# A gated recurrence and its feed-forward on one core: two-batch chunks, crossbar transposes a step earlier, and unequal weight slices

## Chip, cores and metric

The kernel runs on one core of a Trainium2 chip. The core has five engines with a queue each, executed in order: TensorE (PE, matmuls), VectorE (DVE), ScalarE (ACT), GpSimd (POOL) and SyncE (SP, which here only issues transfers). Sixteen DMA engines move data between memory and the core. The metric is the device time of one execution in microseconds (us), lower being better.

## What is computed

Two stages, one feeding the other. The first is a linear attention with a forget gate: for each of 4 batches and 8 heads, a 48 x 48 state is decayed row by row and updated at each of 768 positions, and read out by q. The second is a gated feed-forward without a bias, on rows of 8 x 48 = 384 values, with 1536 hidden units.

```python
f = 1.0 / (1.0 + np.exp(-f_logit))
for t in range(S):                       # S = 768
    state = f[:, :, t, :, None] * state + np.einsum('bhd,bhe->bhde', k[:, :, t], v[:, :, t])
    y[:, :, t] = np.einsum('bhd,bhde->bhe', q[:, :, t], state)
...
gate = np.maximum(x @ w_gate, 0.0)       # x: y as 3072 rows of 384
val = x @ w_val
return (gate * val @ w_out)
```

All inputs and the output are float32; the kernel casts the operands of its matmuls to bf16.

## The kernel before

**Attention in steps.** The 768 positions are cut into 6 steps of 128 (`c` = 0 to 5), and each step is done for the four batches `b` = 0 to 3. `attention(c, b)` works as follows. ACT turns the gate logits into logarithms (L570 and L573, two batches at a time). PE forms their running sums with a triangular matrix (L580, and the sum over the step at L582). ACT takes exponentials of them in both signs (L589, L591) and of the total (L595). POOL multiplies k and q by these, which gives the "hats" (L600, L603), and casts v into a padded tile (L556). The hats lie with positions on partitions and are needed the other way round. For steps below `first_xbar_qk` PE transposes them (L613, eight 128 x 128 transposes into one PSUM bank, copied out by DVE at L619); from that step on SP issues a transposing DMA through the crossbar (L622). Step 0 has a path of its own, `first_pair`. Then PE forms the scores (L636), DVE masks them (L642), and PE forms the output, from the old state (L671) and from the masked scores and v (L675). ACT copies it out (L689). It is transposed to xT by PE (L697, step 2 and below) or by DMA (L705, step 3 and above). PE forms the update of the state (L716), and DVE and POOL apply it (L730, L732).

**Feed-forward in chunks.** `ffn_hidden(c, b0, b1, j)` does one of 12 blocks of 128 hidden units for the batches b0 to b1 of step c: three matmuls for the gate, three for the value (both L748, with 128 columns per batch), a relu on ACT (L755) and a product on DVE (L759). `ffn_out` does the output rows of a batch: 12 matmuls (L770), a copy on ACT (L782) and a store by SP (L785). Which batches go together is listed in `groups`: (step, first batch, last batch, whether outputs follow at once). In the kernel before, step 1 goes in two chunks, and the others from step 2 on in one chunk of four batches, hence 512 columns per matmul. Step 0 is written out ahead of that loop: the weights come in `wsteps` = 3 slices of 4 blocks, and for each slice the two halves of the batches are done.

**Transfers.** SP issues all loads of f, k, q and v (L397, from step 1 on two batches in one load of 393 KB, in rows of 48 floats), the crossbar transposes and the stores, in one queue. POOL issues the loads of the weights, which cast to bf16 (L417). The list `early` fixes the order of the first loads and slices; each may wait until an earlier one of the other kind has landed. Inputs have three buffers (`NL`), so a load of step c waits for the use of step c - 3.

**The order.** Nothing is ordered by hand beyond that. All operations are recorded with `add`, with a cost (`occ`: the engine is taken; `lat`: until the result is there) and a priority, and `Plan.schedule` lists them on each engine by simulating these costs. Feed-forward matmuls have a low priority (1000 is added), so they fill PE wherever attention isn't ready by the plan. `settled` and `margin` add 0.5 us (PE) or 0.6 us (SP) to the readiness of what depends on other engines after 40 us of planned time, feed-forward matmuls excepted. Transfers have a planned flow (0.9 us per batch of a load, 1.06 per hat transpose). The plan only fixes orders: on the chip each engine runs its list and waits on semaphores. `NWARM` = 100 matmuls on zeros (L453) fill PE until the first feed-forward matmul.

Of the kernel before, what the change touches and what calls it, by code (L numbers as in the profile page):

```python
# [43 lines left out]
class Plan:  # L44
# [4 lines left out]
    def __init__(self, limits):  # L49
        self.ops = []  # L50
        self.limits = limits
        self.settled, self.margin = 0.0, {}

    def add(self, eng, emit, reads=(), writes=(), occ=0.5, lat=0.2, prio=0, opens=(), after=(), follows=(),
            paced=()):
# [39 lines left out]
    def schedule(self, banks):  # L95
# [25 lines left out]
        while left:  # L121
            pick = None
            for e in self.ENGINES:
                for op in waiting[e]:
                    at = max(free[e], op.ready)
                    slot = ()
                    if op.opens:
                        slot = banks_for(op)
                        if slot is None:
                            continue  # L130
                        at = max(at, slot[-1]["at"])
                    key = (at, op.prio, op.idx)
                    if pick is None or key < pick[0]:
                        pick = (key, op, slot)
            if pick is None:
                raise RuntimeError("no op can be scheduled: " + repr(
                    [(e, len(waiting[e])) for e in self.ENGINES]))
            (at, _, _), op, slot = pick
            e = op.eng
            waiting[e].remove(op)  # L140
            if op.ends:
                gone = {o for o in self.ops if o.filler and o.start is None}
                waiting["PE"] = [o for o in waiting["PE"] if o not in gone]
                self.ops = [o for o in self.ops if o not in gone]
                left -= len(gone)
            for tile, s in zip(op.opens, slot):
                if s["tile"] is not None:
                    for o in s["tile"].ops:
                        op.deps[o] = "war"
                s["tile"] = tile  # L150
                tile.ap, tile.slot = s["ap"], s
                used[tile.group] = used.get(tile.group, 0) + 1
            op.start, op.end = at, at + op.occ + op.lat
            if op.flow is not None:
                backlog = max(flow_free - op.end, 0.0)
                flow_free = op.end + backlog + op.flow
                op.end += op.flow + op.late + (min(backlog, op.flow) if op.ring == "own" else backlog)
            free[e] = at + op.occ
            op.pos = len(order[e])
            order[e].append(op)  # L160
            left -= 1
            for t in {t for t in op.reads + op.writes if isinstance(t, Bank)}:
                if all(o.start is not None for o in t.ops):
                    t.slot["at"] = max(o.end for o in t.ops)
                    used[t.group] -= 1
            for u in op.users:
                u.n_left -= 1
                if u.deps[op] == "order":
                    at = op.start
                elif u.eng == op.eng == "PE":  # L170
                    at = op.start + op.occ
                else:
                    at = op.end
                    if at > self.settled and (u.eng != "PE" or u.prio < 1000):
                        at += self.margin.get(u.eng, 0.0)
                u.ready = max(u.ready, at)
                if u.n_left == 0:
                    waiting[u.eng].append(u)
# [50 lines left out]
def bass_hgrn2_outer__then__ffn_reglu_kernel(  # L229
# [7 lines left out]
    w_out: bass.AP,  # L237
    out: bass.AP,
):
    wsteps = 3  # L240
    early = ("f0.0.1 f0.1.2 f0.2.3 f0.3.4 k0.0.1 k0.1.2 q0.0.1 q0.1.2 v0.0.1 v0.1.2 k0.2.3 k0.3.4 "
             "q0.2.3 q0.3.4 v0.2.3 v0.3.4 wg0 wv0 wg1 wv1 wg2 wv2 f1.0.2 k1.0.2 q1.0.2 v1.0.2 wo0 wo1 "
             "wo2 f1.2.4 k1.2.4 q1.2.4 v1.2.4").split()
    lag = 4.0
    first_xbar_qk = 3
    flight = 3
    WP = 0
    NWARM = 100
    split_first = 1
    late = 2.5  # L250
    spread_engines = ['ACT', 'DVE', 'ACT', 'ACT']
# [2 lines left out]
    first_xbar_x = 3  # L254
    load_batches = 2
    hat_engines = ['DVE', 'POOL']
    groups = [(0,0,4,1),(1,0,2,0),(1,2,4,0),(2,0,4,0),(3,0,4,0),(4,0,4,0),(5,0,4,0)]
    B, H, S, D = q.shape
    C = 128
    NC = S // C  # L260
# [2 lines left out]
    NK = HD // 128  # L263
# [52 lines left out]

    pl = Plan({"bc": 1, "tp": 1, "s": 2, "y": 1, "kv": 1, "f": 4, "w": 1})
    pl.settled, pl.margin = 40.0, {"PE": 0.5, "SP": 0.6}
    add = pl.add
    gp, ve, sc, te, sy = nc.gpsimd, nc.vector, nc.scalar, nc.tensor, nc.sync  # L320

# [31 lines left out]
        ["ident"], ["ident"], occ=0.3, prio=-8)  # L353
    add("POOL", lambda: gp.memset(ones[:], 1.0), [], ["ones"], occ=0.1, prio=-8)

    def zero(eng, e, t, name, cols, prio):
        add(eng, lambda: e.memzero(t), [], [name], occ=0.15 + cols / 2000.0, prio=prio)  # L357

    zero("DVE", ve, zeros[:], "zeros", 128, -20)
    for i in range(NB):  # L360
        zero("DVE", ve, bneg[i][:], f"bneg{i}", 1024, -9)
    for i in range(NH):
# [20 lines left out]
    def load(n, c, b0, b1, after=(), paced=(), eng="SP"):  # L383
        last = tails.get("load" + eng)
        e = sy if eng == "SP" else sc
        t = ld[n][c % NL]
        src = bass.AP(tensor=srcs[n].tensor, offset=b0 * H * S * D + c * C * D,
                      ap=[[D, C], [S * D, (b1 - b0) * H], [1, D]])
        dst = t[:, b0:b1, :, :].rearrange("p b h d -> p (b h) d")
        flow = 0.9 * (b1 - b0)  # L390
        if c == 0 and n != "v":
            u = b0 % 2
            src = bass.AP(tensor=srcs[n].tensor, offset=b0 * H * S * D, ap=[[2 * D, 64], [S * D, H], [1, 2 * D]])
            dst = t[64 * u:64 * u + 64, b0 - u:b0 - u + 2, :, :].rearrange("p b h d -> p (b h d)").rearrange(
                "p (h x) -> p h x", h=H)
            flow = 0.82
        op = add(eng, lambda: e.dma_start(dst, src), [], [f"{n}{c % NL}_{b}" for b in range(b0, b1)],  # L397
                 occ=(0.8 if eng == "SP" else 0.3) * (b1 - b0) * (0.8 if c == 0 else 1), lat=2.0 if c == 0 else 0.9, prio=c * 100 - 150 * (eng != "SP"), after=after,
                 follows=[last] if last else [], paced=paced)
        tails["load" + eng] = op  # L400
        dma(op, f"{n}{c % NL}_{b0}{b1}", flow, (6.0 if (c, n, b0) == (1, "v", 0) else 2.0) if c else 0.8)
        return op

    WJ = NJ // wsteps
    wsrc = {"wg": w_gate, "wv": w_val}

    def load_w(nm, s, after, landed=()):
        if nm == "wo":
            src = bass.AP(tensor=w_out.tensor, offset=s * WJ * 128 * DM,
                          ap=[[DM, 128], [128 * DM, WJ], [1, DM]])  # L410
            dst = wo[:, s * WJ:(s + 1) * WJ, :]
        else:
            src = bass.AP(tensor=wsrc[nm].tensor, offset=s * WJ * 128,
                          ap=[[DFF, 128], [128 * DFF, NK], [1, WJ * 128]])
            dst = (wg if nm == "wg" else wv)[:, :, s * WJ * 128:(s + 1) * WJ * 128]
        last = tails.get("load_w")
        op = add("POOL", lambda: gp.dma_start(dst, src), [], [f"{nm}{s}"], occ=0.8, lat=1.0, prio=WP, paced=after,  # L417
                 after=landed, follows=[last] if last else [])
        tails["load_w"] = op
        dma(op, f"{nm}{s}", 6.3 / wsteps)  # L420
        return op


# [26 lines left out]

    cold = Bank("w")
    for i in range(NWARM):
        op = add("PE", lambda: te.matmul(cold.ap[:, 0:256], zeros[:, 0:128], zeros[:, :]), ["zeros"], [cold], occ=0.22 if i < 17 else 0.11,  # L453
                 lat=PE_L, prio=1000000, opens=[cold] if i == 0 else [])
        op.filler = True

# [279 lines left out]
    def ffn_hidden(c, b0, b1, j):  # L736
# [8 lines left out]
        def proj(bank, wt):  # L745
            def run():
# [2 lines left out]
                                   start=(kt == 0), stop=(kt == NK - 1))  # L749
                return mm  # L750
            return run
        op = chain("ffn", "PE", proj(gate, wg), xk + [f"wg{j // WJ}"], [gate], occ=pe_t(n, n, n), lat=PE_L,
              prio=P + 1000, opens=[gate])
        op.ends = count["h"] == 1
        add("ACT", lambda: sc.activation(relu[ri][:, 0:n], gate.ap[:, 0:n], AF.Relu), [gate], [f"relu{ri}"],  # L755
            prio=P, **act_t(n))
        chain("ffn", "PE", proj(val, wv), xk + [f"wv{j // WJ}"], [val], occ=pe_t(n, n, n), lat=PE_L,
              prio=P + 1000, opens=[val])
        add("DVE", lambda: ve.tensor_tensor(gT[gi][:, j, n0:n1], relu[ri][:, 0:n], val.ap[:, 0:n], ALU.mult),  # L759
            [val, f"relu{ri}"], [f"gT{gi}_{j}_{b}" for b in range(b0, b1)], prio=P, **dve_t(n))  # L760
# [1 line left out]
    def ffn_out(g, *bs):  # L762
# [11 lines left out]
        for s in range(NJ // OJ):  # L774
            js = range(s * OJ, (s + 1) * OJ)
            for o, b in zip(outs, bs):
                P = (g + 1) * B * 10 + 5 + NJ * 3 + b * 3
                chain("ffn", "PE", proj_out(o, b, s), [f"gT{gi}_{j}_{b}" for j in js] + sorted({f"wo{j // WJ}" for j in js}),
                      [o], occ=pe_t(*[DM] * OJ), lat=PE_L, prio=P + 1000, opens=[o] if s == 0 else [])
        for o, b in zip(outs, bs):  # L780
            oi, P = (g * B + b) % NO, (g + 1) * B * 10 + 5 + NJ * 3 + b * 3
# [5 lines left out]
            dma(op, f"osb{oi}", 0.45)  # L787

    OJ = 4
    OPAIR = 2  # L790
    count = {"h": 0}
    sent = {x[1:] for x in early if x[0] != "w"}
# [3 lines left out]
    for c in range(NC):  # L796
# [7 lines left out]
        for b in range(B):  # L804
            attention(c, b)
        if c == 0 and split_first:
            for s in range(wsteps):
                for b0 in (0, 2):
                    for j in range(s * WJ, (s + 1) * WJ):
                        ffn_hidden(0, b0, b0 + 2, j)  # L810
            for b in range(0, B, OPAIR):
                ffn_out(0, *range(b, b + OPAIR))
# [92 lines left out]
```

## Time and profile before

| | before |
|---|---|
| time, median of 3 (lowest to highest) | 202.8 us (201.86 to 203.2) |
| profiled span | 198.9 us |
| busy: PE, ACT, DVE, POOL | 192.1, 115.1, 107.0, 77.2 us |
| loads of f, k, q, v from issue to landing, medians | 5.2 to 5.8 us |
| transpose of hats by DMA, issue to landing, median | 3.9 us |
| granted TensorE clock | 1.000 |

The profiled execution is a separate one, and its span is counted from its first to its last instruction, so it lies below the timed executions. Busy PE time counts overlapping matmuls once, but the end of a matmul is modelled; what a matmul costs in a row of others is read from the distance between starts. A row of the timeline gives the start, the length, the engine, the line and operation, the tiles written and read, and in brackets the engine's idle time before it with what ended it.

### The profile page before, as it was taken

How to read it: one execution, taken by the hardware profiler on the slowest of the kernel's cores; microseconds unless marked ns; L12 is line 12 of the kernel's file. 1: busy time of each engine (PE TensorE's matmuls, PEld its weight loads, DVE VectorE, ACT ScalarE, POOL GpSimd, SP SyncE). 2: the span in 40 equal slices, each digit the busy share in tenths (PEclk: the TensorE clock that was granted, in tenths of full speed). 3: DMA queues.
4: the chain of work that ended last, by engine and by line, in shares of the span. 5: the costliest groups of instructions: out<-in, count | busy, mean ns of one | idle time of the engine just before them, and what ended most of it. 6: DMA issues, size and time to landing. Idle time of an engine off the chain costs nothing.

```text
span 198.9 us, 4530 instructions
## 1 busy us (share of the span) xinstructions
PE 192.1 (97%) x1796; PEld 122.9 (62%) x1796; DVE 107.0 (54%) x208; ACT 115.1 (58%) x263; POOL 77.2 (39%) x111
## 2 busy tenths in 40 slices
PE   7999999999999999999997989999999999999994
PEld 5887588866888787745553535555545555544552
DVE  7258865574399787647737443636265233443300
ACT  2786767906888677867649466386425433344311
POOL 5189303733859668693573174504500000000000
PEclk9999999999999999999999999999999999999999
DMA  4999999999979999999798899988942200111112
GB/s 118 232 225 198 201 214 187 209 222 243 254 173 227 193 240 177 198 212 207 158 213 167 174 185 202 215 171 187 190 112 59 63 31 9 40 40 43 40 71 87
DMA packets 118180, 31.74 MB, mean 160 GB/s; under 512 B 111248, under 2 KB 118160, under 8 KB 118160
## 3 DMA queue, kind: packets, MB, share of 16 engines
q1 hardware_dynamic: 114176, 27.93, 70.3%
q0 software_dynamic: 3984, 3.54, 11.2%
q8 instruction: 14, 0.23, 0.5%
q14 instruction: 6, 0.05, 0.1%
HBM read 25.95 MB, written 4.72 MB: 154 GB/s over the span
## 4 chain that ended last, share of the span: by engine, by line
PE 78%; DMA 10%; SPq 5%; ACT 3%; POOL 2%; issue 1%
PE ps L748 43%; PE ps L770 22%; SPq L397 4%; DMA wv<-in_moe_w_val_dram 4%; PE ps L636 3%; DMA q_in<-in_q_dram 3%; DMA f_in<-in_f_logit_dram 2%; DMA k_in<-in_k_dram 2%; PE ps L613 2%; PE ps L675 2%; PE ps L716 2%; PE ps L671 2%; PE ps L580 1%; ACT relu L755 1%; POOL hats L603 1%; PE ps L582 1%
## 5 line engine op out<-in xcount | busy, mean ns | idle before, releaser
L759 DVE TENSOR_TENSOR gT<-relu,ps 128x256 bf16<-128x256 bf16 (+1 forms) x96 | 52.1, 551 | 59.1 <-PE ps L748 41.4
L748 PE MATMUL ps<-xT,wv 128*128 128x256 bf16 (+1 forms) x288 | 62.5, 326 | 0.5 <-DMA wv<-in_moe_w_val_dram 0.5
L748 PE MATMUL ps<-xT,wg 128*128 128x256 bf16 (+1 forms) x288 | 62.5, 326 | 0.1
L755 ACT ACTIVATE relu<-ps 128x256 bf16<-128x256 f32 (+1 forms) x96 | 46.0, 490 | 27.6 <-PE ps L748 27.3
L770 PE MATMUL ps<-wo,gT 128*128 128x384 bf16 x288 | 52.2, 326 | 0.0
L770 PEld LDWEIGHTS ps<-wo,gT 128*128 128x128 bf16 x288 | 26.6, 97 | 16.8
L748 PEld LDWEIGHTS ps<-xT,wv 128*128 128x128 bf16 x288 | 26.1, 97 | 16.6 <-DMA wv<-in_moe_w_val_dram 0.6
L642 DVE TENSOR_TENSOR ptm<-ps,tri 128x512 bf16<-128x512 f32 x48 | 31.0, 684 | 9.8 <-PE ps L636 9.6
L748 PEld LDWEIGHTS ps<-xT,wg 128*128 128x128 bf16 x288 | 26.6, 98 | 15.2 <-DMA xT<-xn 0.8
L782 ACT ACTIVATE osb<-ps 128x384 f32<-128x384 f32 x24 | 11.7, 491 | 31.7 <-PE ps L770 31.7
L600 POOL TENSOR_TENSOR hats<-k_in,expo 128x384 bf16<-128x384 f32 x20 | 19.9, 997 | 17.6 <-ACT expo L589 17.6
L603 POOL TENSOR_TENSOR hats<-q_in,expo 128x384 bf16<-128x384 f32 x20 | 19.8, 998 | 11.2 <-DMA q_in<-in_q_dram 11.2
L732 POOL TENSOR_TENSOR st<-ssum,dec 128x384 bf16<-128x384 f32 x16 | 13.2, 829 | 14.6 <-DVE ssum L730 14.6
L453 PE MATMUL ps<-zeros 128*128 128x256 bf16 x96 | 14.3, 307 | 1.1 <-DVE zeros L357 1.1
L689 ACT ACTIVATE xn<-ps 128x384 bf16<-128x384 f32 x20 | 9.8, 490 | 6.0 <-PE ps L675 6.0
L556 POOL CAST vpad<-v_in 128x384 bf16<-128x384 f32 x24 | 12.1, 518 | 2.3 <-DMA v_in<-in_v_dram 2.2
L589 ACT ACTIVATE expo<-ps 128x384 f32<-128x384 f32 x20 | 9.8, 491 | 4.0 <-PE ps L582 3.8
L453 PEld LDWEIGHTS ps<-zeros 128*128 128x128 bf16 x96 | 10.1, 110 | 3.2 <-DVE zeros L357 1.1
L570 ACT ACTIVATE f_in<-f_in 128x768 f32<-128x768 f32 x10 | 8.4, 838 | 4.4 <-DMA f_in<-in_f_logit_dram 4.4
L730 DVE TENSOR_TENSOR ssum<-ps,st 128x384 f32<-128x384 f32 x16 | 8.8, 551 | 2.7 <-PE ps L716 2.6
L636 PE MATMUL ps<-qkT 48*128 48x128 bf16 x192 | 9.5, 219 | 0.6 <-DMA qkT<-hats 0.6
L591 ACT ACTIVATE expo<-ps 128x384 f32<-128x384 f32 x20 | 9.9, 495 | 0.0
(71 smaller groups left out, 153.5 us busy)
## 6 DMA issues: line engine op xcount, KB each, us to landing
out_dram<-osb SPq DMA_DIRECT2D x24, 192.0 KB, 2.2
f_in<-in_f_logit_dram SPq DMA_DIRECT2D x10, 384.0 KB, 5.8
k_in<-in_k_dram SPq DMA_DIRECT2D x10, 384.0 KB, 5.2
q_in<-in_q_dram SPq DMA_DIRECT2D x10, 384.0 KB, 5.4
v_in<-in_v_dram SPq DMA_DIRECT2D x10, 384.0 KB, 5.4
wg<-in_moe_w_gate_dram POOLq DMA_DIRECT2D x3, 384.0 KB, 7.2
wv<-in_moe_w_val_dram POOLq DMA_DIRECT2D x3, 384.0 KB, 7.4
wo<-in_moe_w_out_dram POOLq DMA_DIRECT2D x3, 384.0 KB, 7.3
```

The costliest lines, as they stand in the source:

```text
L453: op = add("PE", lambda: te.matmul(cold.ap[:, 0:256], zeros[:, 0:128], zeros[:, :]), ["zeros"], [cold], occ=0.22 if i < 17 else 0.11, lat= ...
L556: add("POOL", lambda: gp.tensor_copy(vout, vin[:, b, :, :].rearrange("p (n j) d -> p n j d", j=2)), [f"v{li}_{b}", f"vpad{vi}"], [f"v_{vi} ...
L600: add("POOL", lambda: gp.tensor_tensor(hk, kin[:, b, :, :], ex[:, 1, :].rearrange("p (h d) -> p h d", h=H), ALU.mult), [f"k{li}_{b}", f"ex ...
L603: add("POOL", lambda: gp.tensor_tensor(hq, qin[:, b, :, :], ex[:, 0, :].rearrange("p (h d) -> p h d", h=H), ALU.mult), [f"q{li}_{b}", f"ex ...
L636: mm = te.matmul(s.ap[:, p * C:(p + 1) * C], qkT[qi][lo:lo + D, 1, p, :], qkT[qi][lo:lo + D, 0, p, :])
L642: add("DVE", lambda j=j, s=s: ve.tensor_tensor(ptm[mi][:, j, :, :], s.ap[:, :].rearrange("p (n t) -> p n t", n=NP), mask, ALU.mult), [s, " ...
L732: add("POOL", lambda: gp.tensor_tensor(t4(s_new), t4(tmp), rate, ALU.mult), [key] + dk, [f"S{b}_{c % 2}"], prio=P + 8, **pool_t(HD))
L748: mm = te.matmul(bank.ap[:, 0:n], wt[:, kt, j * 128:(j + 1) * 128], xT[xi][:, kt, n0:n1], start=(kt == 0), stop=(kt == NK - 1))
L755: add("ACT", lambda: sc.activation(relu[ri][:, 0:n], gate.ap[:, 0:n], AF.Relu), [gate], [f"relu{ri}"], prio=P, **act_t(n))
L759: add("DVE", lambda: ve.tensor_tensor(gT[gi][:, j, n0:n1], relu[ri][:, 0:n], val.ap[:, 0:n], ALU.mult), [val, f"relu{ri}"], [f"gT{gi}_{j}_ ...
L770: mm = te.matmul(o.ap[:, 0:DM], gT[gi][:, j, b * C:(b + 1) * C], wo[:, j, :], start=(j == 0), stop=(j == NJ - 1))
L782: add("ACT", lambda o=o, oi=oi: sc.activation(osb[oi][:, :], o.ap[:, 0:DM], AF.Copy), [o], [f"osb{oi}"], prio=P, **act_t(DM))
```

## The change

It does five things. The feed-forward of steps 2 and 3 is cut into two chunks of two batches, as that of step 1 was. The q and k hats of step 2 are transposed by the DMA crossbar (`first_xbar_qk` 3 to 2), so that PE and DVE are free of them. The gate and value weights are loaded in slices of 2, 2, 4 and 4 blocks, so that the first matmuls need less data, while the feed-forward of step 0 runs by six blocks per half (`JB`). The planner's margin for PE is doubled after 85 us of planned time. Some planned costs differ: a load takes SP 0.6 us per batch and not 0.8, and the zeros that the warm-up reads are planned to come later.

```diff
-                        at += self.margin.get(u.eng, 0.0)
+                        at += self.margin.get(u.eng, 0.0) + (self.more if at > self.later and u.eng == "PE" else 0.0)
...
-    wsteps = 3
...
-             "q0.2.3 q0.3.4 v0.2.3 v0.3.4 wg0 wv0 wg1 wv1 wg2 wv2 f1.0.2 k1.0.2 q1.0.2 v1.0.2 wo0 wo1 "
-             "wo2 f1.2.4 k1.2.4 q1.2.4 v1.2.4").split()
+             "q0.2.3 q0.3.4 v0.2.3 v0.3.4 wg0 wv0 wg1 wv1 wg2 wv2 wg3 wv3 f1.0.2 k1.0.2 q1.0.2 v1.0.2 "
+             "wo0 wo1 wo2 f1.2.4 k1.2.4 q1.2.4 v1.2.4").split()
...
-    first_xbar_qk = 3
+    first_xbar_qk = 2
...
-    groups = [(0,0,4,1),(1,0,2,0),(1,2,4,0),(2,0,4,0),(3,0,4,0),(4,0,4,0),(5,0,4,0)]
+    groups = [(0,0,4,1),(1,0,2,0),(1,2,4,0),(2,0,2,0),(2,2,4,0),(3,0,2,0),(3,2,4,0),(4,0,4,0),(5,0,4,0)]
...
+    pl.later, pl.more = 85.0, 0.5
...
-    zero("DVE", ve, zeros[:], "zeros", 128, -20)
+    zero("DVE", ve, zeros[:], "zeros", 128, -20, 0.9)
...
-                 occ=(0.8 if eng == "SP" else 0.3) * (b1 - b0) * (0.8 if c == 0 else 1), lat=2.0 if c == 0 else 0.9, prio=c * 100 - 150 * (eng != "SP"), after=after,
+                 occ=(0.6 if eng == "SP" else 0.3) * (b1 - b0) * (0.8 if c == 0 else 1), lat=2.0 if c == 0 else 0.9, prio=c * 100 - 150 * (eng != "SP"), after=after,
...
-    WJ = NJ // wsteps
+    w_cuts = {"wg": [int(x) for x in ['0', '2', '4', '8', '12']], "wo": [0, 4, 8, 12]}
+    w_cuts["wv"] = w_cuts["wg"]
+
+    def w_slice(nm, j):
+        return f"{nm}{sum(x <= j for x in w_cuts[nm]) - 1}"
...
+    JB = 6
...
-            for s in range(wsteps):
+            for j0 in range(0, NJ, JB):
                 for b0 in (0, 2):
-                    for j in range(s * WJ, (s + 1) * WJ):
+                    for j in range(j0, j0 + JB):
                         ffn_hidden(0, b0, b0 + 2, j)
```

More of the change, by code (lines that the diff above doesn't have):

```diff
@@ L51, in __init__ @@
         self.limits = limits
-        self.settled, self.margin = 0.0, {}
+        self.settled, self.margin, self.later, self.more = 0.0, {}, 0.0, 0.0
     def add(self, eng, emit, reads=(), writes=(), occ=0.5, lat=0.2, prio=0, opens=(), after=(), follows=(),
@@ L248, in bass_hgrn2_outer__then__ffn_reglu_kernel @@
     NWARM = 100
+    NCOLD = 17
     split_first = 1
@@ L354, in bass_hgrn2_outer__then__ffn_reglu_kernel, with zero @@
     add("POOL", lambda: gp.memset(ones[:], 1.0), [], ["ones"], occ=0.1, prio=-8)
-    def zero(eng, e, t, name, cols, prio):
-        add(eng, lambda: e.memzero(t), [], [name], occ=0.15 + cols / 2000.0, prio=prio)
-    zero("DVE", ve, zeros[:], "zeros", 128, -20)
+    def zero(eng, e, t, name, cols, prio, lat=0.2):
+        add(eng, lambda: e.memzero(t), [], [name], occ=0.15 + cols / 2000.0, lat=lat, prio=prio)
+    zero("DVE", ve, zeros[:], "zeros", 128, -20, 0.9)
     for i in range(NB):
@@ L397, in load @@
         op = add(eng, lambda: e.dma_start(dst, src), [], [f"{n}{c % NL}_{b}" for b in range(b0, b1)],
-                 occ=(0.8 if eng == "SP" else 0.3) * (b1 - b0) * (0.8 if c == 0 else 1), lat=2.0 if c == 0 else 0.9, prio=c * 100 - 150 * (eng != "SP"), after=after,
+                 occ=(0.6 if eng == "SP" else 0.3) * (b1 - b0) * (0.8 if c == 0 else 1), lat=2.0 if c == 0 else 0.9, prio=c * 100 - 150 * (eng != "SP"), after=after,
                  follows=[last] if last else [], paced=paced)
         tails["load" + eng] = op
-        dma(op, f"{n}{c % NL}_{b0}{b1}", flow, (6.0 if (c, n, b0) == (1, "v", 0) else 2.0) if c else 0.8)
+        dma(op, f"{n}{c % NL}_{b0}{b1}", flow, (6.0 if (c, n, b0) == (1, "v", 0) else 2.0 if c < 3 else 2.0) if c else 0.8)
         return op
-    WJ = NJ // wsteps
+    w_cuts = {"wg": [int(x) for x in ['0', '2', '4', '8', '12']], "wo": [0, 4, 8, 12]}
+    w_cuts["wv"] = w_cuts["wg"]
+    def w_slice(nm, j):
+        return f"{nm}{sum(x <= j for x in w_cuts[nm]) - 1}"
     wsrc = {"wg": w_gate, "wv": w_val}
     def load_w(nm, s, after, landed=()):
+        j0, j1 = w_cuts[nm][s:s + 2]
         if nm == "wo":
-            src = bass.AP(tensor=w_out.tensor, offset=s * WJ * 128 * DM,
-                          ap=[[DM, 128], [128 * DM, WJ], [1, DM]])
-            dst = wo[:, s * WJ:(s + 1) * WJ, :]
-        else:
-            src = bass.AP(tensor=wsrc[nm].tensor, offset=s * WJ * 128,
-                          ap=[[DFF, 128], [128 * DFF, NK], [1, WJ * 128]])
-            dst = (wg if nm == "wg" else wv)[:, :, s * WJ * 128:(s + 1) * WJ * 128]
+            src = bass.AP(tensor=w_out.tensor, offset=j0 * 128 * DM, ap=[[DM, 128], [128 * DM, j1 - j0], [1, DM]])
+            dst = wo[:, j0:j1, :]
+        else:
+            src = bass.AP(tensor=wsrc[nm].tensor, offset=j0 * 128,
+                          ap=[[DFF, 128], [128 * DFF, NK], [1, (j1 - j0) * 128]])
+            dst = (wg if nm == "wg" else wv)[:, :, j0 * 128:j1 * 128]
         last = tails.get("load_w")
@@ L419, in load_w @@
         tails["load_w"] = op
-        dma(op, f"{nm}{s}", 6.3 / wsteps)
+        dma(op, f"{nm}{s}", 6.3 * (j1 - j0) / NJ)
         return op
@@ L452, in bass_hgrn2_outer__then__ffn_reglu_kernel @@
     for i in range(NWARM):
-        op = add("PE", lambda: te.matmul(cold.ap[:, 0:256], zeros[:, 0:128], zeros[:, :]), ["zeros"], [cold], occ=0.22 if i < 17 else 0.11,
+        op = add("PE", lambda: te.matmul(cold.ap[:, 0:256], zeros[:, 0:128], zeros[:, :]), ["zeros"], [cold], occ=0.22 if i < NCOLD else 0.11,
                  lat=PE_L, prio=1000000, opens=[cold] if i == 0 else [])
@@ L751, in proj @@
             return run
-        op = chain("ffn", "PE", proj(gate, wg), xk + [f"wg{j // WJ}"], [gate], occ=pe_t(n, n, n), lat=PE_L,
+        op = chain("ffn", "PE", proj(gate, wg), xk + [w_slice("wg", j)], [gate], occ=pe_t(n, n, n), lat=PE_L,
               prio=P + 1000, opens=[gate])
@@ L756, in ffn_hidden @@
             prio=P, **act_t(n))
-        chain("ffn", "PE", proj(val, wv), xk + [f"wv{j // WJ}"], [val], occ=pe_t(n, n, n), lat=PE_L,
+        chain("ffn", "PE", proj(val, wv), xk + [w_slice("wv", j)], [val], occ=pe_t(n, n, n), lat=PE_L,
               prio=P + 1000, opens=[val])
@@ L777, in ffn_out @@
                 P = (g + 1) * B * 10 + 5 + NJ * 3 + b * 3
-                chain("ffn", "PE", proj_out(o, b, s), [f"gT{gi}_{j}_{b}" for j in js] + sorted({f"wo{j // WJ}" for j in js}),
+                chain("ffn", "PE", proj_out(o, b, s), [f"gT{gi}_{j}_{b}" for j in js] + sorted({w_slice("wo", j) for j in js}),
                       [o], occ=pe_t(*[DM] * OJ), lat=PE_L, prio=P + 1000, opens=[o] if s == 0 else [])
```

## Prediction

> **What bounds the kernel now.** I read the busy rows and slices of the page first, then the chain of waits, the waits by engine, the windows, and last the timelines of PE and of SP's queue.
>
> ```profile
> PE 192.1 (97%) x1796; PEld 122.9 (62%) x1796; DVE 107.0 (54%) x208; ACT 115.1 (58%) x263; POOL 77.2 (39%) x111
> ...
> DMA  4999999999979999999798899988942200111112
> ...
> DMA packets 118180, 31.74 MB, mean 160 GB/s; under 512 B 111248, under 2 KB 118160, under 8 KB 118160
> ...
> PE 78%; DMA 10%; SPq 5%; ACT 3%; POOL 2%; issue 1%
> ```
>
> Two resources are full at once. PE is busy 97% of the span, and the 16 DMA engines are at nine tenths from slice 2 to slice 29 (145 us). So PE's work is one floor, and the rate at which inputs arrive is another until 145 us. After that there is only feed-forward work: the DMA row is nearly empty, and PE runs alone to 196 us. DVE, ACT and POOL are half idle.
>
> ```profile
> 50.00:100.00 50.00, 50.00 (x594) 36.27 (x592) 36.24 (x74) 37.70 (x104) 35.29 (x44) 1.00 1.08 204
> 100.00:145.00 45.00, 42.72 (x355) 22.31 (x354) 22.10 (x35) 26.45 (x54) 19.40 (x25) 1.00 0.96 188
> 145.00:198.90 53.90, 51.02 (x302) 26.54 (x300) 17.86 (x27) 19.40 (x35) 0.00 (x0) 1.00 0.16 52
> ```
>
> In the windows view (PE first, DMA share and GB/s last) PE never idles from 50 to 100 us, and loses about 2.3 us from 100 to 145. The PE timeline says where:
>
> ```profile
> 22.18 0.50 PE L748 MATMUL ps<-xT,wv 128*128 128x256 bf16 x3 [0.47 <-DMA wv<-in_moe_w_val_dram]
> ...
> 105.60 0.34 PE L580 MATMUL ps<-bneg,tri 128*128 128x384 bf16 x1 [0.64 <-ACT bneg L573]
> ...
> 109.27 0.40 PE L636 MATMUL ps<-qkT 48*128 48x128 bf16 x8 [0.60 <-DMA qkT<-hats]
> ...
> 116.13 0.34 PE L716 MATMUL ps<-vpad,hats 128*128 128x96 bf16 x4 [0.94 <-POOL vpad L556]
> ```
>
> All three late waits end behind a load that came late; by the distance between starts they cost about 3.1 us. The wait at 22 us is for the first slice of w_val. SP's own timeline shows that its issues take 1.5 to 4 us each while the transfers are backed up, against 0.4 us when they are not:
>
> ```profile
> 55.02 3.73 SPq L397 DMA_DIRECT2D f_in<-in_f_logit_dram  x1
> 58.80 1.52 SPq L397 DMA_DIRECT2D k_in<-in_k_dram  x1
> 60.43 1.78 SPq L397 DMA_DIRECT2D q_in<-in_q_dram  x1
> 62.26 2.61 SPq L397 DMA_DIRECT2D v_in<-in_v_dram  x1
> ```
>
> **What the Trainium skill says.** "Advanced Engine Details and Errata", section X-Bar Transpose (TRN2), holds that a crossbar transpose is as fast as an ordinary DMA, 350 to 400 GB/s. One transpose of hats moves 128x1024 bf16, 262 KB, so that would be 0.7 us (an estimate). In this trace, counted from the landing ahead of it, it takes 0.92 to 1.73 us (four back to back ones: 0.92, 0.94, 1.02, 1.03); I use the trace. "DMA: Bandwidth & Descriptors", Issuing engines are not separate DMA queues, says that transfers of all queues share the same 16 engines: a transpose put there takes time from the loads, and the SP rows above agree. The same page, Why small descriptors are slow (HBM only), explains why the loads are dear: rows of 48 floats are 192 bytes, and 111248 of 118180 packets lie under 512. A load of two batches (393 KB) lands 1.64 to 1.86 us after the one ahead where nothing else stands between: about 225 GB/s. "TensorE: Matmul & The Clock Gate", Back-to-back issue gap, gives N/2.4 + 2.5 ns: 109 for 256 columns, 216 for 512. The trace agrees: 96 matmuls in 10.59 us (0.1103), 18 in 3.88 us (0.2156).
>
> **The change, part by part.**
> Step 2's q and k hats leave PE. Four times eight transposes of 56 ns (0.45 us per batch at L613) go: -1.8 us of PE. The four copies L619 go too, 4 x 684 ns of DVE, which nothing waited for at its average of half idle.
> In exchange DMA gets four transposes, 4 x 1.1 us (both ends: 1.0 and 1.6), and SP four issues of about 1.3 us. This falls between 62 and 80 us, where DMA is full, so all later transfers shift by it. On SP a transpose waits for its hats, and queued behind it are the loads of step 3 and an output store; who waits for those is the attention of step 3.
> Splitting steps 2 and 3 into two chunks (step 1 was split before) turns 144 matmuls of 512 columns into 288 of 256: 288 x 0.1103 - 144 x 0.2156 = +0.7 us (+0.4 with the 109 and 216 ns of the skill). ACT pays 2 x (24 x 383 - 12 x 596) ns = 4.1 us, DVE 2 x (24 x 417 - 12 x 686) = 3.6 us, against its 2.7 saved. Both are hidden by PE's matmuls: from 50 to 80 us PE already ran the split step 1 without a gap. What the split buys: feed-forward may start once two batches are through, so PE has other work while a late load is awaited.
> PE's total is thus -1.1 to -1.4 us.
> Weights in slices of 2, 2, 4, 4: the first w_val slice is half as long and is issued right behind w_gate's, so it lands before 20 us instead of 22.13: the 0.5 us wait goes. But there are two more issues on POOL at 0.8 us; hats of the second pair and the last two v casts wait behind them. The first chunk now goes by six blocks, so block 4 needs the third w_val slice, which like the second slice of before (same bytes ahead of it) lands near 26.0, about half a microsecond late. On DVE the third q hat moves ahead of the first mask, and its load lands only at 15.94, where the mask began at 15.54: the first xT is about 0.5 to 1 us later. Sum of the start: between -0.7 and +0.7; I take 0.
> Eight fewer warm-up matmuls (0.9 us) stand ahead of the first cumulative sum, which waited for them (ACT was done at 6.92, PE came at 8.2); but the next step waited for q_in until 10.67, which hides it. Costs and margins of the planner cost nothing themselves; they move the order.
> The order is the larger part. After the scores of step 5, batch 1, PE has 61.3 us of matmuls left in the new order and 57.7 in the old (counted from the two instruction orders, at 0.109, 0.216 and 0.162 us per matmul of 256, 512 and 384 columns and 0.025 to 0.056 for the small ones). So attention stands some 3.6 us earlier in PE's work, and PE, without any wait, would be at these scores at 127 us; in before it was there at 137.16. The question is whether DMA can feed that.
> DMA count: the second q load of step 2 landed at 66.5 us, and nothing ahead of it changes much. Behind it the new SP order has, up to the transpose for step 5, batch 1: 24 loads x 1.75 + 14 hat transposes x 1.1 + 7 xT transposes x 0.48 + 7 stores x 0.5 = 64.3 us, so 130.8 us. PE waits some 4 us in all, spread over steps 2 to 5. From there: 0.45 (these scores) + 61.3 + 0.7 of small gaps (before had 0.7 by the same count) + 2.9 (store after PE's end, 198.9 - 196.0) = 196.2 us of span. Times lie 3.9 above the profiled span (202.8 - 198.9): **200.1**.
>
> **The rivals.**
> *DMA is never smooth, and its holes decide: slower.* In before the same count for the second q load of step 4 gives about 106 us where it landed at 113.6: 8 us were holes, in which SP stood at a transpose or store whose data were not ready. In the new order more transposes stand among the loads. For it: SP is one queue; against it: PE came late there because it was planned late, and a queue that is behind finds its data ready. With 1.85 us per load and 1.4 per transpose, or five to six us of holes, the scores come at about 136.5: 205.8.
> *DMA keeps up.* At 1.7 and 1.0 the scores come at 128; PE is the only floor: 197.3. For it: 254 GB/s is reached in one slice, against 225 assumed.
> *A wash.* Two to three us of holes eat the 2.7 us: 202.6. For it: the saved PE work is under 1% and the waits of before (3.1 us) are replaced by others of the same size.
>
> **How the numbers follow.** Forecast (199 to 200.7) 0.36, DMA keeps up 0.17, a wash 0.28, holes 0.19. A time under 200.8 is over 1% faster: 0.36 + 0.17 = 0.53. The wash, 200.8 to 204.8, is 0.28. Slower is 0.19. The predicted time is 200.1; the range reaches from 197.0 into the slower case, 205.3, which leaves out about 0.1 at the top and somewhat less below.
>
> **What would show it.** Right: PE without transposes of hats from 57 us on, first w_val matmuls without a wait, DMA at nine tenths to 145 us or longer, PE waits of about 4 us behind loads and hat transposes between 65 and 130 us, scores of step 5, batch 1 near 131. Wrong: those scores after 134 (holes, or dearer transposes), a wait for weights of over 1 us near 25 us, or PE waiting for ACT or DVE in the split steps.

## The result and the profile after

The changed kernel takes 213.9 us (median of 4 runs, 212.7 to 214.7) against 202.4 us: a ratio of 1.056, interval 1.049 to 1.063. It is slower, and outside the range that was given. Some executions of a kernel take over 1.5% longer than its fastest; the times below are medians of the others, and the ratios compare those alone.

The profiled span went from 198.9 to 213.0 us. These are single executions: that of before took 200.7 us, less than its median, and that of the changed kernel 214.7, more than its median, so the spans differ by 14.1 us where the medians differ by 11.5. Differences of two to three us between two traces are for this reason not read as effects of an edit. The page's busy rows and slices of the changed kernel:

```profile
PE 191.2 (90%) x1903; PEld 134.3 (63%) x1903; DVE 106.6 (50%) x228; ACT 117.5 (55%) x287; POOL 78.8 (37%) x113
...
DMA  5999999999999999999999799899922010111112
...
DMA packets 123207, 32.83 MB, mean 154 GB/s; under 512 B 115504, under 2 KB 123184, under 8 KB 123184
```

PE's busy time fell by 0.9 us, and its share fell from 97% to 90%: the longer span is idle time of PE. The DMA row is full as before, over a stretch that ends some 8 us later (slices are 5.3 us wide here). The windows that were shown of before, with the last ending at the new span:

```profile
50.00:100.00 50.00, 46.85 (x574) 36.89 (x573) 30.00 (x69) 35.88 (x100) 32.65 (x41) 1.00 1.13 206
100.00:145.00 45.00, 34.99 (x392) 25.72 (x390) 21.05 (x46) 24.43 (x68) 18.85 (x23) 1.00 1.01 182
```

PE idles 3.2 us from 50 to 100 us, where it had no gap, and 10 us from 100 to 145, where it had 2.3. The DMA share is as high as in before, and the rate no higher (182 GB/s against 188). What PE waits for (engine, line, who it waits for; us in total, times, longest):

```profile
PE ps L642 <- DMA qkT<-hats: 7.8, 5, 2.6
PE ps L722 <- POOL vpad L562: 2.1, 2, 1.2
PE ps L522 <- DVE hats L512: 1.8, 1, 1.8
PE ps L776 <- DMA wo<-in_moe_w_out_dram: 1.3, 1, 1.3
```

L642 are the scores (L636 before). The same row of before:

```profile
PE ps L636 <- DMA qkT<-hats: 0.6, 1, 0.6
```

So they waited 0.6 us for a hat transpose, in one place, and now 7.8 in five. The casts of v behind the second row waited for v loads. The third row is the start, the fourth the third slice of w_out, which was issued at 38.02 us instead of 35.87. Some waits for ACT stand further down the list; they too end at a late load. ACT works through its list in order, and there a relu stood behind a load of f that had not landed:

```profile
111.36 0.84 ACT L576 ACTIVATE f_in<-f_in 128x768 f32<-128x768 f32 x1 [3.61 <-DMA f_in<-in_f_logit_dram]
112.11 0.36 ACT L761 ACTIVATE relu<-ps 128x256 bf16<-128x256 f32 x1
...
112.53 0.50 PE L754 MATMUL ps<-xT,wv 128*128 128x256 bf16 x3 [1.17 <-ACT relu L761]
```

One account holds for all kernels below. The last scores of step 5 come right behind the last inputs; behind them PE's list runs through (its idle time there is 0.3 us or less in each of them). So PE's end is the time of the last scores plus what the list has behind them:

| | last v load lands | last scores | behind them | PE ends |
|---|---|---|---|---|
| before | 141.7 | 149.7 | 46.3 | 196.0 |
| changed | 149.9 | 156.3 | 53.8 | 210.1 |

The change loses on both terms: data came 8.2 us later, and PE's list had put 7.5 us more of its work behind the last scores. The second term is no cost by itself, since the work has to be done in any case; it tells how much PE had left undone while it waited.

### The profile page after: what moved, and what is told of

It is laid out like the page before. It is cut to its first block, busy times and chain, and to the rows that moved or that the text cites. A ratio compares the mean times of both kernels' runs of the same rounds, so it can differ in the third digit from the quotient of the medians.

```text
span 213.0 us, 4826 instructions
## 1 busy us (share of the span) xinstructions
PE 191.2 (90%) x1903; PEld 134.3 (63%) x1903; DVE 106.6 (50%) x228; ACT 117.5 (55%) x287; POOL 78.8 (37%) x113
## 4 chain that ended last, share of the span: by engine, by line
PE 55%; DMA 19%; SPq 12%; ACT 7%; POOL 3%; issue 2%; DVE 1%
PE ps L754 30%; PE ps L776 16%; SPq L398 5%; DMA f_in<-in_f_logit_dram 5%; DMA qkT<-hats 5%; SPq L628 5%; DMA wo<-in_moe_w_out_dram 3%; DMA v_in<-in_v_dram 3%; DMA q_in<-in_q_dram 3%; ACT relu L761 2%; PE ps L642 2%; SPq L711 2%; PE ps L722 1%; ACT f_in L576 1%; ACT bneg L579 1%
## 5 line engine op out<-in xcount | busy, mean ns | idle before, releaser
L765 DVE TENSOR_TENSOR gT<-relu,ps 128x256 bf16<-128x256 bf16 (+1 forms) x120 | 54.3, 470 | 58.5 <-ACT relu L761 29.5
L754 PE MATMUL ps<-xT,wv 128*128 128x256 bf16 (+1 forms) x360 | 66.7, 294 | 2.1 <-ACT relu L761 1.2
L761 ACT ACTIVATE relu<-ps 128x256 bf16<-128x256 f32 (+1 forms) x120 | 49.9, 429 | 31.9 <-PE ps L754 31.1
L754 PE MATMUL ps<-xT,wg 128*128 128x256 bf16 (+1 forms) x360 | 66.6, 294 | 0.4 <-DVE xT L707 0.4
L754 PEld LDWEIGHTS ps<-xT,wv 128*128 128x128 bf16 x360 | 33.3, 98 | 14.7 <-ACT relu L761 1.4
L754 PEld LDWEIGHTS ps<-xT,wg 128*128 128x128 bf16 x360 | 33.6, 98 | 12.2 <-DVE xT L707 0.7
L642 PE MATMUL ps<-qkT 48*128 48x128 bf16 x192 | 9.5, 218 | 7.8 <-DMA qkT<-hats 7.8
L459 PE MATMUL ps<-zeros 128*128 128x256 bf16 x91 | 12.8, 294 | 1.1 <-DVE zeros L358 1.1
L642 PEld LDWEIGHTS ps<-qkT 48*128 48x128 bf16 x192 | 5.5, 94 | 11.9 <-issue 6.6
L595 ACT ACTIVATE expo<-ps 128x384 f32<-128x384 f32 x20 | 9.9, 496 | 2.3 <-PE ps L588 2.0
L459 PEld LDWEIGHTS ps<-zeros 128*128 128x128 bf16 x91 | 9.2, 105 | 2.6 <-DVE zeros L358 1.1
```

The costliest lines, as they stand in the source:

```text
L642: mm = te.matmul(s.ap[:, p * C:(p + 1) * C], qkT[qi][lo:lo + D, 1, p, :], qkT[qi][lo:lo + D, 0, p, :])
L754: mm = te.matmul(bank.ap[:, 0:n], wt[:, kt, j * 128:(j + 1) * 128], xT[xi][:, kt, n0:n1], start=(kt == 0), stop=(kt == NK - 1))
```

## Experiments

`a` marks an edit of the changed kernel, `b` an edit of the kernel before. Ratios are to the kernel before on the same chip, with 95% intervals. The expectations name the theories that a run is to tell apart. COUNT: each transpose through the crossbar costs by itself. ALTERNATION: what costs is that loads and transposes take turns in SP's queue. SPLIT: the smaller feed-forward chunks cost. ORDER: PE's list has attention ahead of its data.

### Which part

**a_qk_back** (`first_xbar_qk` back to 3).

> The changed kernel with the hats of step 2 transposed by PE again; all else as changed. Theory COUNT (four more transposes on the crossbar cost about 3 us each): about 202 to 203 us. Theory ALTERNATION (what is dear is that nearly every load has a transpose right ahead of it in SP's queue, an effect of the planned 0.6 us per load, and steps 3 to 5 keep that order): 207 to 209. Theory SPLIT (the smaller feed-forward chunks hold PE up through ACT): 212 or more.

211.0 us, 1.042 (1.032 to 1.052). Without the four transposes the last v load lands at 142.5, 7.4 us earlier than in the changed kernel, so their cost in DMA is real. But the time falls by 3 us only: the last scores are at 149.9, as in before, and 57.4 us stand behind them. COUNT alone doesn't fit, and ALTERNATION gave less; SPLIT's figure is the nearest, and b_split below tests it. Part of the time is a slower clock, of which the last section tells.

**a_load08** (one number).

```diff
-                 occ=(0.6 if eng == "SP" else 0.3) * (b1 - b0) * ...
+                 occ=(0.8 if eng == "SP" else 0.3) * (b1 - b0) * ...
```

> The changed kernel with a load's planned cost on SP back at 0.8 us per batch, which puts loads and transposes in longer runs of one kind and attention later in PE's list; all else as changed. ALTERNATION: 203 to 207 us, fewer loads that land over 2 us after the transfer ahead. COUNT: 212 or more, since the same transposes run. SPLIT: 212 or more.

209.5 us, 1.035 (1.027 to 1.043). Better by 4 us than the changed kernel with the same transposes, so COUNT alone is out. But data did not come earlier, as ALTERNATION would have it: the last v load lands at 153.6, 3.7 us later. What is better is the list, which has 42.1 us behind the last scores and not 53.8.

**b_qk_xbar** (`first_xbar_qk` 3 to 2 alone).

> The kernel before with the hats of step 2 on the crossbar, nothing else. COUNT: about 212 us. ALTERNATION: 203 to 206, since the order of before keeps runs of loads. SPLIT: 201 to 203.

206.4 us (two executions), 1.023 (1.013 to 1.032): just above ALTERNATION's range and far below COUNT's. The edit that takes 1.8 us off PE costs some 4.6.

**b_split** (`groups` of the change alone).

> The kernel before with the feed-forward of steps 2 and 3 in two chunks, nothing else. SPLIT: 208 us or more. COUNT and ALTERNATION: 201 to 204 (0.4 to 0.7 us more of matmuls against fewer waits between 100 and 116 us).

204.9 us, 1.016 (1.010 to 1.023), just above COUNT's and ALTERNATION's range and below SPLIT's. PE has 45.3 us behind the last scores, 1.0 less than before; but these come at 154.5, and the last v load lands 4.0 us later than before. Splitting moves stores, and with them SP's list. ACT by its own work isn't the cause that SPLIT named: PE waits 0.2 us for it, and once 1.4 us for a product on DVE whose relu stood on ACT behind a late load of f, as shown above.

**b_slices** (slices of 2, 2, 4, 4 and `JB` = 6 alone) and **b_zeros** (the zeros' latency alone).

> The kernel before with the weight slices of 2, 2, 4 and 4 blocks and the runs of six blocks in step 0, nothing else. If the start is a cost of its own (in the changed kernel PE idles 1.9 us ahead of the third set of transposes, since the q load of batches 2 and 3 lands 0.7 us later beside the earlier weights): 203 to 205 us, with step 1's first scores 1 us or more later than at 41.6 us. If the start costs nothing: 201 to 203.

202.5 us, 1.001 (0.998 to 1.005).

> The kernel before with the zeros of the warm-up planned to come 0.7 us later, nothing else; PE's list then has 37, 7 and 8 warm-up matmuls ahead of the first steps where it had 43, 21 and 5. If these lists of warm-up matmuls are what made the changed kernel's start late: 203 to 205 us and first scores of step 1 later than 42.3 us (41.6 in before). If it was the weights' earlier start: 201.5 to 203, first scores near 41.6.

202.1 us, 1.002 (0.999 to 1.005). Neither costs anything alone. In b_zeros step 1's first scores came at 42.65, as in the changed kernel, 1.0 us later than before, and that is nearly all filled up again later.

**b_load06** (the same number as in a_load08, 0.8 to 0.6, alone).

> The kernel before with a load planned at 0.6 us of SP per batch instead of 0.8, nothing else: the lists of SP and PE then have step 5's scores some 10 us of PE work earlier, and loads and transposes take turns. ORDER and ALTERNATION: 205 to 209 us. If only the added transposes matter: 201 to 203.

210.6 us, 1.048 (1.035 to 1.062), a little over the forecast: almost the whole loss of the change, from one planned cost that no instruction has. The transfers end when they did: the last v load lands at 141.6 (before: 141.7), the last scores are even 2.7 us earlier, at 147.0. But 59.0 us stand behind them instead of 46.3. PE's timeline shows it waiting where before it did feed-forward:

```profile
105.68 0.34 PE L580 MATMUL ps<-bneg,tri 128*128 128x384 bf16 x1 [1.99 <-ACT bneg L573]
...
133.17 0.34 PE L580 MATMUL ps<-bneg,tri 128*128 128x384 bf16 x1 [3.33 <-ACT bneg L573]
```

ACT had waited for f_in. The planner believed that loads come faster, listed attention earlier, and listed the feed-forward that could have filled the wait behind it.

**b_more** (the added margin alone).

> The kernel before with the further 0.5 us of PE margin after 85 us of planned time, nothing else. PE's list then has step 5's last scores 3.6 us of PE work earlier (49.7 us left behind them, against 46.1). ORDER: if DMA brings them at 147 to 150 us as before, 202 to 206.

202.8 us, 1.008 (1.005 to 1.011). Data as before (last v load 141.2), last scores at 147.6, 49.9 us behind: the same effect, small.

### What makes the data late

**a_plain.** The sixteen hat transposes as plain transfers; the kernel leaves the transposing out.

```diff
-    sy.dma_start(qkT[qi].rearrange("p x n t -> p (x n) t"), hats[hi]..., transpose=True)
+    sy.dma_start(qkT[qi].rearrange("p x n t -> p (x n t)"), hats[hi]...)
```

> The changed kernel with the sixteen crossbar transposes of hats replaced by plain transfers of the same 262 KB in the same place of SP's queue, so what attention computes from step 2 on is not the reference's. TRANSPOSE (a transpose starts only when the load ahead of it is through, and the load behind it starts late): the time falls to 200 to 205 us, and a load behind one of these transfers lands about 1.8 us after it instead of 2.4. BYTES (the 4 x 262 KB themselves fill the DMA engines): 211 to 215, as the changed kernel.

204.4 us, 1.012 (1.008 to 1.015). All lists and all bytes are the same; of the 5.6% only 1.2% are left, and the last v load lands at 139.0 instead of 149.9. PE's waits for hats fall from 7.8 to 1.5 us:

```profile
PE ps L522 <- DVE hats L512: 1.5, 1, 1.5
PE ps L642 <- DMA qkT<-hats: 1.5, 2, 0.8
```

So BYTES is out. From 50 to 150 us a load behind one of these transfers lands 1.83 us after it (median of 11), against 2.43 in the changed kernel, as TRANSPOSE had it. SP's issues behind a load, though, stay long:

```profile
63.04 2.23 SPq L628 DMA_DIRECT2D qkT<-hats  x1
65.32 0.59 SPq L398 DMA_DIRECT2D v_in<-in_v_dram  x1
65.96 2.73 SPq L628 DMA_DIRECT2D qkT<-hats  x1
```

The same rows of the changed kernel:

```profile
62.74 2.27 SPq L628 DMA_TRANSPOSE qkT<-hats  x1
65.06 0.58 SPq L398 DMA_DIRECT2D v_in<-in_v_dram  x1
65.68 3.40 SPq L628 DMA_TRANSPOSE qkT<-hats  x1
```

so the length of an issue is mostly the queue's backing up, not the transpose.

**b_load06_plain.** b_load06 with all 24 transposes, of hats and of x, as plain transfers.

> The kernel before with loads planned at 0.6 us per batch and all 24 crossbar transposes (hats and x) replaced by plain transfers of the same bytes, so attention and feed-forward from step 3 on are not the reference's. If the crossbar is what keeps DMA from following the early list: the last v load lands near 132 us instead of 141.6, and the time falls from 211.9 to 198 to 203. If DMA's rate for the loads alone keeps it back: 208 or more.

199.7 us, 0.990 (0.987 to 0.993). The last v load lands at 129.0, the last scores are at 136.2, and the same 59.0 us behind them end at 195.2. PE's window that lost 9.3 us in b_load06 loses none; first b_load06, then this kernel:

```profile
100.00:145.00 45.00, 35.70 (x314) 19.22 (x317) 20.18 (x32) 23.50 (x49) 18.82 (x24) 1.00 0.93 186
```

```profile
100.00:145.00 45.00, 45.00 (x402) 24.84 (x399) 24.83 (x39) 27.18 (x56) 17.61 (x22) 1.00 0.78 184
```

With plain transfers the early list costs nothing. (The kernel before with plain transfers was not run, so whether the early list would then be the better one isn't shown.) The DMA share is lower here, 0.78 against 0.93, at nearly the same rate, 184 and 186 GB/s: a full DMA row did not mean that as many bytes as possible were moved.

**a_pairs** and **b_pairs**: the hats of two batches come first, then their two transposes back to back.

```diff
-    [f"hk{hi}", f"hq{hi}"], qk_key, ...
+    [f"hk{hi}", f"hq{hi}"] + ([f"hk{(hi + 1) % NH}", f"hq{(hi + 1) % NH}"] if b % 2 == 0 else []), qk_key, ...
```

> The changed kernel with the hat transposes of two batches issued one right behind the other: the first waits for the hats of both. ALTERNATION: 206 to 209 us, since half of the turns between load and transpose go. COUNT: 212 to 215.

209.6 us, 1.036 (1.028 to 1.044). Four us better than the changed kernel, and just above ALTERNATION's range. But its reason isn't ALTERNATION's: the last v load lands at 149.7, as in the changed kernel, although 10 loads stand behind a transpose where 15 did. The gain is again in the list, with 48.6 us behind the last scores.

> The kernel before with the hat transposes of two batches issued one behind the other. ALTERNATION: 200 to 202 us, since before already has most of them with few loads between. If the wait for both batches' hats costs as much as it saves: 202 to 205.

201.7 us, 0.999 (0.995 to 1.002): no difference.

**h_sp06**: SP's list from the plan at 0.6, the other engines' from the plan at 0.8.

> The kernel before with SP's list taken from the plan at 0.6 us per load, and the lists of PE, ACT, DVE and POOL from its own plan at 0.8. ORDER (what costs is PE's list, which has attention ahead of the data): 201 to 204 us. ALTERNATION (what costs is SP's list, in which loads and transposes take turns): 206 to 212, as with both lists (211.9).

206.4 us, 1.023 (1.014 to 1.032). SP's list alone has about half of what both have (4.8%), so ORDER by PE's list is not all. Only the times of this run are used. Whether turns in SP's list cost, or that its list no longer fits those of the other engines, isn't shown, and PE's list alone was not run.

### Towards a better plan

**a_true_cost** (a planned flow of 2.4 us per hat transpose, in place of 1.06).

> The changed kernel with a planned flow of 2.4 us per hat transpose instead of 1.06, which is about what one costs with the slower load behind it; PE's list then has attention of steps 3 to 5 some 5 to 15 us later. ORDER (PE loses its time because its list has attention ahead of what DMA can deliver, while other work was there): 203 to 207 us. LIMIT (DMA's rate itself sets the end): 211 or more.

209.2 us, 1.034 (1.026 to 1.042). PE waits 0.3 us in all from 82 to 140 us, and has 39.0 us behind the last scores, but these come at 166.1: PE ran out of other work at 141 us and waited 3.6 us, and twice 1.6 us soon after. For a while it also had a slower clock (column before the last two):

```profile
135.00:145.00 10.00, 6.11 (x80) 4.49 (x78) 4.38 (x9) 5.07 (x11) 3.70 (x5) 0.96 0.96 199
145.00:155.00 10.00, 6.84 (x49) 3.46 (x48) 3.27 (x5) 2.73 (x6) 4.79 (x6) 0.53 0.85 161
155.00:165.00 10.00, 9.94 (x66) 4.91 (x65) 4.92 (x8) 4.45 (x8) 0.00 (x0) 1.00 0.32 73
```

A later list doesn't mend late data; it moves the wait to the end.

**b_qk4** (`first_xbar_qk` 3 to 4: eight crossbar transposes of hats).

> The kernel before with the hats of step 3 transposed by PE as well, so 8 crossbar transposes of hats instead of 12, nothing else. If one costs about 1.2 us of the end, as 12 to 16 did: PE pays 1.8 us and the waits of before between 100 and 116 us (3.1 us) go, 199 to 201.5 us. If the trade is even at 12: 202 to 204, PE's added work.

203.3 us, 1.009 (1.006 to 1.012). The last v load lands at 138.0, 3.7 us earlier, but PE pays 1.8 us of transposes and the list has 57.7 us behind the last scores. Twelve, as in the kernel before, is the better number for this planner.

**b_load10** (a load planned at 1.0).

> The kernel before with a load planned at 1.0 us of SP per batch: PE's list has step 5's scores 5 us of PE work later than before. ORDER: DMA sets the last scores near 150 us or the list does, 5 us later, with 5 us less left behind: 201 to 204 us, no gain, since PE waits for little in before; the cost is one-sided.

201.0 us, 0.998 (0.996 to 1.001). One-sided, as expected: 0.6 costs 4.8%, 1.0 nothing.

**b_pairs_load10** (both).

> The kernel before with both edits that came out a little under it: hat transposes issued in pairs, and a load planned at 1.0 us of SP per batch. ORDER and ALTERNATION together: PE's waits of before (3.1 us between 100 and 116 us) fall to about 1 us, 199 to 201 us against 201.4 to 202. If each was noise: 201 to 203.

201.1 us, 0.998 (0.995 to 1.002). No run with the whole computation beat the kernel before by more than its interval.

## Why the prediction was wrong

**PE's work: right.** By the distance between starts, 32 transposes took 1.8 us off, and the 288 short matmuls cost 0.4 more than the 144 long ones: -1.4 us, the end of the stated range. The gap formula that was cited stands in the Trainium skill, "TensorE: Matmul & The Clock Gate", Back-to-back issue gap, for a matmul by itself; for streams of 512 columns the page has 131 ns. The streams of this trace took 0.2156 us each, so here the formula holds and the page's figure for streams doesn't.

**The start: worse than its range.** Slices and zeros alone are worth nothing, as forecast. In the changed kernel the first w_val matmuls did not wait; the third set of transposes did, since the q load of batches 2 and 3 landed at 16.66 instead of 15.94. Step 1's first scores came 1.0 us later. The 1.3 us for the third w_out slice was not foreseen: POOL's list had a k hat ahead of its issue.

**The split: too cheap.** Its matmuls cost what was said, but SP's list moved with it, and b_split lost 1.6%. Which of SP's moves does it wasn't isolated. That ACT's and DVE's added work is hidden held only as long as loads came in time: in the changed kernel PE waits 2.2 us for ACT and 0.8 us for a product on DVE, and in before for neither there.

**The order: taken for a gain, and it was the loss.** "Attention stands some 3.6 us earlier in PE's work" was counted right. It is a gain only if data keep up. The step chosen to decide that was the DMA count, and it failed. From the second q load of step 2 (66.18 us, forecast 66.5) to the transpose of step 5, batch 1 it gave 64.3 us; the chip took 81.6, and these scores came at 147.85 us and not at 130.8. By the landings in the changed kernel's trace, each counted from the landing ahead:

| | forecast | measured |
|---|---|---|
| 24 loads | 42.0 | 55.9 |
| 14 hat transposes | 15.4 | 15.7 |
| 7 xT transposes | 3.4 | 6.4 |
| 7 stores | 3.5 | 3.5 |

The mis-sized term is the load. The 1.75 us came from loads behind loads, and so it still is (five, mean 1.63). But 14 of the 24 loads now stood behind a transpose and landed 2.45 us after it in the mean, and 5 behind a store, 2.68. Before had 8 loads behind a transpose from 50 to 150 us, at a median of 2.20: the number was there to be read.

This doesn't make turns the cause. What a transpose takes shows when a fixed stretch is timed, here from the landing of that q load to the landing of the last v load, with 25 loads in every kernel:

| | hat transposes in it | loads behind a transpose | us |
|---|---|---|---|
| b_qk4 | 6 | 8 | 69.6 |
| before | 10 | 8 | 75.2 |
| b_load06 | 10 | 12 | 73.8 |
| a_true_cost | 14 | 6 | 87.3 |
| a_pairs | 14 | 10 | 83.5 |
| changed | 14 | 15 | 83.7 |
| a_plain | 14, plain | 15 | 72.0 |

The time goes with the number of hat transposes and not with the turns. Eight more of them add 14.1 us, about 1.8 us each (an estimate from the first and the sixth row), where the count had 1.1. The landing of a transpose shows only part of this; the rest falls on whatever lands next. So COUNT had the right cause for the data, at 1.8 us and not 3; ALTERNATION isn't borne out, and the gains of a_load08 and a_pairs came from PE's list.

**The 8 us that were set aside.** In before they were read as time in which SP stood at a transpose or store whose data weren't ready. The trace shows otherwise. From 66.5 to 113.6 us SP stands 1.5 us in all between its issues, 0.8 of it at a store and none at a transpose. The excess lies in the landings: the 16 loads took 33.1 us where the prices give 28.0, and the 4 stores 4.3 instead of 2.0. In the changed kernel SP stands 0.4 us from 66.2 to 147.8. So the argument that a queue that is behind finds its data ready was true, and no help: the slow part was the transfers themselves, and a list that calls for the data earlier can't hasten those. b_load06 agrees: PE's list called for them some 10 us earlier, and the last v load landed at the same 141.6.

**The rival "its holes decide" had the direction**, and neither the cause nor the size: 5 to 6 us were allowed for, and 17 came. With the 8 us seen in before carried over into the count, the forecast would have come much nearer.

**The last terms.** Behind those scores the sum held: PE ended 62.2 us later. But the 3.9 us between timed and profiled executions are no property of the kernel. The profiled execution of before took 200.7 us itself, 1.8 more than its span, and that of the changed kernel 1.7 more. This term hid 3 of the 17 us. And of the four transposes called back to back two stood behind loads and two behind stores; the twelve of before took 1.31 us in the mean. In the changed kernel this made no difference, with 1.12.

**"Planned costs cost nothing themselves; they move the order"** is so, and b_load06 prices the move at 4.8%. The parts add up to more than the whole (4.8 + 2.3 + 1.6 + 0.8% against 5.6%): the parts overlap, as they would when PE waits only once for the same late load.

## What to carry to other kernels

Where one engine's list is fixed ahead, the end is the time of the last transfer-bound step plus what the list has behind it, and an edit that moves such steps forward pays only if transfers keep up. Price a transfer by what a fixed stretch of the queue takes longer with it, and not by the time from the landing ahead of it to its own: here the first is 1.8 us and the second 1.1. A planned cost that was too low was far dearer here than one that was too high (0.6 in place of 0.8 cost 4.8%, 1.0 nothing), since the lists then put attention ahead of its data and the work that could fill the wait behind it. And time that a full queue loses in the trace before belongs into any count of what it can carry, until the trace shows who waited for whom.

## What the runs showed of the hardware

A crossbar transpose of hats hardly differs from a plain transfer of the same 262 KB in its own length: from the first to the last packet 1.57 us in the changed kernel and 1.35 in a_plain (medians from 55 to 140 us, fetches of instructions left out). It differs in what else moves meanwhile. While the packets of a transpose ran, the loads and stores of the queue moved at 35 GB/s in the changed kernel, 19 in before and 29 in b_load06; beside the plain transfers at 85 in a_plain and 91 in b_load06_plain. This is where the time of a load behind a transpose goes; why the crossbar holds the others up is open.

When a fetch of instructions (a packet of 16 KB, one every 10 to 15 us) fell beside a transpose, the transpose often took longer. Over the seventeen kernels with crossbar transposes of hats, 61 had such a packet beside them, and 37 of these took more than 2.2 us, up to 3.57; of the 159 others one did, with 2.28. The changed kernel had four of about 3 us, before two of about 2.5. Plain transfers were drawn out too (in a_plain three of six with a fetch took about 2.6 us, and none of ten without over 1.52), but loads went on moving beside them. That the fetch is cause and not company was not tested by itself.

The clock: a_true_cost ran 10.2 us at half speed from 144.2 us on, about the end of its wait of 3.6 us, and a_qk_back twice 3.4 us, close behind waits of 2.3 and 2.0 us. The second of these may have cost a_qk_back up to 1.7 us (an estimate, half of 3.4). The Trainium skill has this, in "TensorE: Matmul & The Clock Gate", What's actually happening: how busy PE was of late sets how much of its clock is let through. But a wait of 3.3 us in b_load06 had no such effect (its row above has 1.00), nor one of 2.6 us in the changed kernel. The length of a single wait doesn't decide it here, so late data may or may not cost this on top.
